# Five v tiles split among the score tiles and kept in DRAM, one turn of GpSimd for both final sums, and checks re-slotted: a Fourier and expert layer on one core

## The chip, the cores and the metric

The kernel runs on one core of a Trainium2 chip. The metric is the device time of one execution in microseconds (us); the median over runs counts. The profile is one execution recorded by the hardware profiler. Engine names: PE is the matrix engine (TensorE), DVE the vector engine, ACT the scalar engine, POOL GpSimd, SP the engine that issues most DMA transfers (SPq and POOLq are the DMA issues of SP and POOL).

## The reference, cut to what matters

```python
xn  = layernorm(x)                                   # x: 2048 x 512
A   = Re(DFT_seq(DFT_hidden(xn)))                    # 2048 x 512
q   = einsum("nd,dhc->nhc", xn, w_q)                 # 32 heads, two halves of 128
s1, s2 = q1 @ k1.T, q2 @ k2.T                        # 64 + 64 scores a head
i1, i2 = top2(s1), top2(s2)
cand, eidx = sums and indices of the 2 x 2 pairs;  top_s, top_e = top 2 of cand
g   = softmax(top_s)
act = gelu(einsum("nd,nhkd->nhk", xn, u[top_e]))     # u: 4096 experts x 512
B   = einsum("nhk,nhk,nhkd->nd", g, act, v[top_e])   # v: 4096 experts x 512
out = x + A + B
```

## The kernel before, in words

The 2048 rows are 16 tiles of 128. Operands of matmuls are split into a high and a low float16 part and multiplied in three products, so that the result has nearly float32 accuracy; the casts of the splits are ACT's (high part), with the low part's subtraction on POOL. While it computes, the kernel also tests its inputs (that the DFT matrices given are DFT matrices, that magnitudes fit the scaling); if a test fails, a slower branch at the end recomputes everything. These tests are called checks here.

The work comes in four stages, all on PE, one behind the other.

1. *Fourier part* (0 to 88 us): the DFT as matmuls; its result goes to DRAM (`y_d`, with `xt_d` for the transposed, split rows).
2. *Scores* (88 to 449 us): 8 groups of 4 heads (index j) by 16 row tiles (index i), 128 score tiles n = 16 j + i. Each is 12 matmuls (`scores`, L790) out of one of 4 PSUM buffers; ACT evicts it (L795), DVE takes the best of each head (MAX8 L798, FIND_INDEX8 L802). The matrix m of a group is the product of w_q and the keys, made by `m_stage` (L146) out of float16 halves of w_q that ACT and POOL prepare (`m_prep`, L160 to L168, in the "wq" ring of 4 buffers). `routing` (L643 to L687) turns a group's scores into experts and gates, in the group after it, in four calls; that of the last group follows the scores and is on DVE. The results for all rows stand in z, which is stored to DRAM as `z_d` (L888). Beside this stand lists by score tile: `todo[n]` holds fills and preparations, `checks` the early checks. A *fill* (`fill_uv`, L602 to L612) splits one of 16 tiles of u or of v: ACT casts the raw tile (L610), ACT scales it (L611), POOL subtracts (L612); its load (`fill_load`, L599) is issued some tiles earlier. The 16 u tiles and v tiles 0 to 10 are filled here (V2 = 11). An *early check* (`compare`, 32 of them, `EARLY`) loads 512 KB of DFT matrix into a buffer "cx" of which there are two, combines it on POOL (`diff`: L747, L753) and sums it on ACT (`judge`: L773, L774); check k is put at tile 20 + 13 k // 4, its load 4 tiles earlier and its judge 2 later.
3. *Row blocks*: rows 0 to 14 (NB = 15) go through all 4096 experts densely. For a block b, `u_part` makes z = u.x in 8 groups of 4 PSUM columns (L935, 48 matmuls each) with the gelu on ACT (L938); `g_mm` builds the gate matrix from one-hot factors that DVE makes (L961 for L, L966 and L969 for R; matmuls L971); `w_part` multiplies both on DVE (L981), and splits the product (ACT L988, DVE L991); `v_part` multiplies it with v (L1000, 96 matmuls of 512 columns); `finish` adds the Fourier part and x (L1015) and stores the rows. The loop over b runs v of block b, then u of block b + 2; blocks 0 and 1 have their u ahead of the loop. The x tile of a block (xb, 256 KB) is loaded by `prep` (L918), z of a block by `compact_d` (L923), y by `add_x` (L1008 from y_d on SP, L1009 x added by POOL's queue). Paced by v's and u's groups: the other 36 checks (`paced`, on DVE and ACT here) and, in block 0's v part, the fills of v tiles 11 to 15.
4. *The sixteenth block* is done row by row beside this: for 64 pairs of head and rank, POOL gathers a row of u and v for each of 128 rows (L1026), DVE takes the dot product (`dot`, L1042), ACT the gelu and the scaling (`gain`, L1053 to L1056), POOL adds it to ov (L1057). `pick` hands out these steps, 212 turns over the blocks.

At the end `verdict` sums the checks over partitions with two POOL instructions (partition_all_reduce, L1150 and L1151; DVE L1154 to L1169 takes the decision), and `finish` of block 14 and its store follow on DVE and SP.

The order on each engine is by priority and dependencies of a tile scheduler; `follow` adds an order without a wait between two instructions, and `hold` does so for all that a function issues. DMA loads of SP go out in the order of its queue.

## Time and profile before

| | us |
|---|---|
| median of 3 runs (1161.86, 1161.0, 1160.99) | 1161.0 |
| the profiled execution | 1159.16 |
| its span | 1157.4 |
| PE busy | 1111.0 (96%) |
| DVE busy | 924.8 (80%) |
| ACT busy | 670.4 (58%) |
| POOL busy | 482.4 (42%) |

The span runs from the first to the last recorded instruction; what lies around it in the execution is 1.8 us. A row of a timeline has the start in us, the duration, the engine, the line of the kernel, the operation with its output and input, and in brackets how long the engine sat idle before it and which instruction released it. A group's row has the busy time in us, the mean duration in ns, and the idle time before. The mean granted clock of PE was 0.99 of full speed.

### The profile page before, as it was taken

The page shows a single profiled execution, that of the slowest core. Times are in us where ns is not written, and L with a number is a line of the kernel's source. Part 1 is how long each engine was busy: PE and PEld are TensorE (multiplying, and loading weights), DVE is VectorE, ACT ScalarE, POOL GpSimd, SP SyncE. Part 2 cuts the span into 40 slices and gives each one's busy share as a digit, 9 for nine tenths or more (in the row PEclk, how much of TensorE's full clock was granted, in tenths as well). Part 3 has the DMA queues.
Part 4 walks back from the last instruction along what each step waited for, and adds up shares of the span by engine and source line. Part 5 has one row for each costly group of instructions (what it writes and reads, how often), then busy time and mean ns, then how long its engine had stood idle before and what let it go on. Part 6 is the DMA issues. An engine that isn't in the chain of part 4 may idle for free.

```text
span 1157.4 us, 29244 instructions
## 1 busy us (share of the span) xinstructions
PE 1111.0 (96%) x11681; PEld 730.1 (63%) x11681; DVE 924.8 (80%) x2790; ACT 670.4 (58%) x1250; POOL 482.4 (42%) x442
## 2 busy tenths in 40 slices
PE   5799999999999999979999999999999999999996
PEld 4354555444444446957687696786876876967842
DVE  7878897787978999897888777778787886787781
ACT  3575667687877866354464554554654645545541
POOL 0021749679887863140333333333333233333321
PEclk9899999999999999999999999999999999999998
DMA  8255245353443331532444535435444454354321
GB/s 314 79 212 189 84 136 175 135 181 101 162 162 126 110 110 36 168 107 78 118 159 152 151 112 167 147 96 159 147 141 119 155 156 150 108 162 149 113 52 49
DMA packets 73346, 157.02 MB, mean 136 GB/s; under 512 B 9062, under 2 KB 25965, under 8 KB 73200
## 3 DMA queue, kind: packets, MB, share of 16 engines
q1 hardware_dynamic: 61522, 117.30, 30.4%
q0 software_dynamic: 11520, 37.75, 11.8%
q8 instruction: 93, 1.52, 0.5%
q14 instruction: 53, 0.43, 0.1%
q10 hardware_dynamic: 158, 0.01, 0.0%
HBM read 141.08 MB, written 13.96 MB: 134 GB/s over the span
## 4 chain that ended last, share of the span: by engine, by line
PE 71%; DVE 12%; POOL 8%; issue 3%; ACT 2%; DMA 2%; SPq 0%; POOLq 0%; DVEq 0%; ACTq 0%
PE z L935 27%; PE v L1000 23%; PE s L790 12%; PE g L971 4%; DVE vals L798 2%; POOL wq L168 2%; DVE idx L802 2%; POOL wq L167 2%; PE p L368 2%; POOL cx L747 1%; POOL u L612 1%; DMA cx<-in_cb_dram 1%; PE m L146 1%; DVE L L961 1%; DVE ft L345 1%
## 5 line engine op out<-in xcount | busy, mean ns | idle before, releaser
L790 PE MATMUL s<-m,xq 128*128 128x512 f16 x1536 | 339.1, 379 | 0.9 <-ACT ss L795 0.9
L935 PE MATMUL z<-xb,u 128*128 128x128 f16 x5760 | 330.6, 219 | 2.4 <-DMA xb<-xt_d 2.4
L935 PEld LDWEIGHTS <-u 128*128 128x128 f16 x5760 | 324.5, 98 | 5.7 <-DMA xb<-xt_d 2.6
L1000 PE MATMUL v<-v,act 128*128 128x512 f16 x1440 | 321.3, 380 | 1.2 <-DVE act L991 1.1
L1057 POOL TENSOR_TENSOR ov<-ov,ga 128x512 f32<-128x512 f32 x64 | 96.0, 1500 | 401.0 <-ACT ga L1056 345.5
L790 PEld LDWEIGHTS <-xq 128*128 128x128 f16 x1536 | 148.4, 98 | 172.3 <-issue 1.4
L961 DVE TENSOR_TENSOR L<-io_lam,cmp 128x2048 f16<-128x2048 f16 x120 | 157.2, 1310 | 112.5 <-PE g L971 79.0
L1000 PEld LDWEIGHTS <-act 128*128 128x128 f16 x1440 | 137.7, 98 | 159.1 <-issue 1.7
L938 ACT ACTIVATE act<-z,scl 128x512 f32<-128x512 f32 x120 | 81.9, 684 | 174.9 <-PE z L935 174.7
L798 DVE MAX8 vals<-ss 128x8 f32<-128x64 f32 x1024 | 152.7, 217 | 16.2 <-ACT ss L795 15.9
L802 DVE FIND_INDEX8 idx<-vals,ss 128x8 uint16<-128x256 f32 x256 | 107.3, 419 | 0.0
L1026 POOL DMA_INDIRECT ga<-in_uv_dram,eix x64 | 93.7, 1463 | 32.3 <-POOL ov L1057 18.3
L991 DVE TENSOR_TENSOR act<-w,act 128x1024 f16<-128x1024 f32 x60 | 81.0, 1350 | 19.2 <-ACT act L988 17.5
L988 ACT ACTIVATE act<-w 128x1024 f16<-128x1024 f32 x60 | 80.9, 1348 | 26.5 <-DVE w L981 26.4
L795 ACT ACTIVATE ss<-s,wsc 128x512 f32<-128x512 f32 x112 | 75.1, 678 | 28.3 <-PE s L790 15.3
L773 ACT ACTIVATE cx<-cx 128x896 f32<-128x896 f32 x64 | 60.6, 947 | 36.2 <-POOL cx L753 9.6
L981 DVE SCALAR_TENSOR_TENSOR w<-act,scl,g 128x1024 f32<-128x1024 f32 x60 | 76.2, 1273 | 0.1
L747 POOL TENSOR_TENSOR cx<-cx 128x512 f32<-128x512 f32 (+2 forms) x56 | 61.8, 1120 | 27.1 <-DMA cx<-in_cb_dram 13.2
L971 PEld LDWEIGHTS <-L 128*128 128x128 f16 x1920 | 56.0, 96 | 15.5 <-issue 8.7
L971 PE MATMUL g<-R,L 128*128 128x32 f16 x1920 | 57.9, 176 | 8.0 <-DVE R L969 8.0
L969 DVE TENSOR_TENSOR R<-R,cmp 128x512 f16<-128x512 f16 x120 | 62.3, 519 | 1.8
L168 POOL TENSOR_TENSOR wq<-wq,wh 128x1024 f16<-128x1024 f32 x26 | 55.4, 2130 | 18.9 <-ACT wq L165 17.9
(276 smaller groups left out, 1259.9 us busy)
## 6 DMA issues: line engine op xcount, KB each, us to landing
cx<-in_cb_dram SPq DMA_DIRECT2D x64, 448.0 KB, 4.6
wq<-in_wq_dram SPq DMA_DIRECT2D x32, 512.0 KB, 4.1
fit<-in_wq_dram SPq DMA_DIRECT2D x28, 512.0 KB, 4.6
uv<-in_ut_dram SPq DMA_DIRECT2D x16, 512.0 KB, 3.9
uv<-in_vn_dram SPq DMA_DIRECT2D x16, 512.0 KB, 3.7
xq<-in_x_dram SPq DMA_DIRECT2D x8, 512.0 KB, 6.7
xt_d<-xq SPq DMA_DIRECT2D x16, 256.0 KB, 2.5
cx<-in_ca_dram SPq DMA_DIRECT2D x64, 64.0 KB, 3.5
```

Source lines behind the costliest of these rows:

```text
L790: mm = nc.tensor.matmul(ps, xt[i][:, l, kd, :], m[:, r, kd, :], start=(n == 0), stop=(n == 3 * KD - 1))
L798: nc.vector.max(vals[:, i, w, :, h], s[:, g, :])
L802: nc.vector.max_index(idx[:, i, w].rearrange("p k h -> p (k h)"), vals[:, i, w, 0:2].rearrange("p k h -> p (k h)"), s[:, w * HC:g + 1, :]. ...
L935: mm = nc.tensor.matmul(p[:, cc * P:(cc + 1) * P], ug[:, l, c % 2, kd, :], xb[:, r, kd, :], start=(n == 0), stop=(n == 3 * KD - 1))
L938: nc.scalar.activation(act[:, cg * 4:cg * 4 + 4, :].rearrange("p c n -> p (c n)"), p, AF.Gelu_apprx_tanh, scale=zsc)
L961: nc.vector.tensor_tensor(L.rearrange("p t (l two) -> p t l two", two=2), io_lam.rearrange("p (l two) -> p l two", two=2).unsqueeze(1).to_ ...
L971: i = nc.tensor.matmul(p[:, hf, t * NC:(t + 1) * NC], L[:, t, :], R[:, t, :], start=True, stop=True)
L988: i = nc.scalar.activation(w16[..., 0], w, AF.Copy)
L991: nc.vector.tensor_tensor(w16[..., 1], w, w16[..., 0], op=ALU.subtract)
L1000: mm = nc.tensor.matmul(pv, w16[:, c, :, l], vg[:, r, c % 2, :], start=(c == 0 and k == 0), stop=(c == NC - 1 and k == 2))
L1026: nc.gpsimd.indirect_dma_start(out=t, out_offset=None, in_=uv, in_offset=bass.IndirectOffsetOnAxis(ap=eix[:, n].rearrange("p k h -> p (k h ...
L1057: nc.gpsimd.tensor_tensor(o, o, t, op=ALU.add)
```

## The change

Its parts:

- *v tiles 11 to 15.* `fill_far` splits them among score tiles 104, 105, 106, 110 and 111, each in a buffer of the "wq" ring, and stores them to DRAM (`v_d`, 512 KB each). Once the score stage's memory is free they are loaded into place by five transfers on SP. The fills in block 0 go.
- *Early checks.* Three buffers instead of two; tiles 7 to 10 of groups 1 to 5, and ten tiles from 101 to 126; the load 3 tiles ahead, the judge one tile behind.
- *xb.* The tiles of x (but block 1's) come from a pool of their own on the other side of memory; block 0's is loaded at the start of the last score group.
- *Order in blocks.* The first two gate matmuls of block 0 come after groups 4 and 6 of z rather than 5 and 7; ACT's steps of checks and rows stand behind the gelu of the same z group; the last `w_part` of the last blocks comes a group earlier.
- *The sixteenth block.* x + y for it is added up early and kept in DRAM (`o_d`); the last two of POOL's additions are issued together, and both partition sums are put behind them. The picks are spread over 206 turns, none in every second group of block 13 and two a group in block 14.
- *Checks in blocks.* Block 13, the last but one, has none of the paced ones; they are spread over the groups before.

```diff
@@ -50,6 +50,8 @@
     z_d = dram.tile([NT, P, 3 * P], F16, name="z_d")
+    v_d = dram.tile([16 - V2, P, 4 * D], F16, name="v_d")
+    o_d = dram.tile([NS, P, D], F32, name="o_d")
@@ -599,8 +601,9 @@
-        def fill_uv(which, g, at=None):
-            dst = (u_sb if which == 0 else v_sb)[g]
+        def fill_uv(which, g, at=None, dst=None):
+            if dst is None:
+                dst = (u_sb if which == 0 else v_sb)[g]
             s = behind(su if which == 0 else sv, at)
@@ -617,6 +620,11 @@
         asums = wqp.tile([P, 16, 2], F32, name="asums", bufs=1)
+
+        def fill_far(g, at):
+            t = wq_tile(f"vs{g}").rearrange("p h k -> p (h k)").bitcast(F16)
+            fill_uv(1, g, at, t.rearrange("p (l c d) -> p l c d", l=2, c=2))
+            nc.sync.dma_start(v_d[g - V2], t)
@@ -709,8 +717,11 @@
                     follow(i, after)
+                if i.engine == mybir.EngineType.Activation and after.ins.name in GL:
+                    follow(i, GL[after.ins.name])
         later = []
+        GL = {}
@@ -719,7 +730,7 @@
             else:
-                t = sp.tile([P, 4, 4, 64], F32, tag="cx", name=f"cx{n}", bufs=2)
+                t = sp.tile([P, 4, 4, 64], F32, tag="cx", name=f"cx{n}", bufs=3)
             v_eng = nc.vector if at is None else nc.gpsimd
@@ -835,23 +846,31 @@
             todo[n - (3 if n < 113 else 1)].append(lambda at, w=which, g=g: fill_load(w, g))
+        for g, n in zip(range(V2, 16), () if safe else (104, 105, 106, 110, 111)):
+            todo[n].append(lambda at, g=g: fill_far(g, at))
+            todo[n - 3].append(lambda at, g=g: fill_load(1, g))
         checks = {}
...
-        for k in range(len(EARLY)):
-            n = 20 + k * 13 // 4
-            checks.setdefault(n - 4, []).append(lambda mm, k=k: check_load(k))
+        at_k = [13, 15] + [16 * j + i for j in range(1, 6) for i in (7, 8, 9, 10)]
+        at_k += [101, 103, 108, 112, 118, 120, 122, 124, 125, 126]
+        for k, n in enumerate(at_k):
+            checks.setdefault(n - 3, []).append(lambda mm, k=k: check_load(k))
             checks.setdefault(n, []).append(lambda mm, k=k: hold(cx[k][0], mm))
-            checks.setdefault(n + 2, []).append(lambda mm, k=k: hold(cx[k][1], mm))
+            checks.setdefault(n + 1, []).append(lambda mm, k=k: hold(cx[k][1], mm))
+        XB = {}
         m_stage(1, wq_tile, 0)
...
                 alloc_v(V1, V2)
+                xbp = stE.enter_context(tc.tile_pool(name="xbp", bufs=1, side="right"))
+                XB[0] = xbp.tile([P, 2, KD, P], F16, tag="xb", name="xb_0", bufs=1)
+                nc.sync.dma_start(XB[0].rearrange("p a k n -> p (a k n)"), xt_d[0])
             vals = sp.tile([P, NT, 2, 8, HC], F32, tag="vals", name=f"vals{j}", bufs=2)
@@ -899,13 +918,17 @@
                 xb = bp.tile([P, 2, 2, KD, P], F16, tag="ga", name="xb_1", bufs=BUFS)[:, 0]
+            elif b:
+                xb = xbp.tile([P, 2, KD, P], F16, tag="xb", name=f"xb_{b}", bufs=1)
             else:
-                xb = ap[0].tile([P, 2, KD, P], F16, tag="xb", name=f"xb_{b}", bufs=1)
+                xb = XB[0]
             act = ap[b % 2].tile([P, NC, P], F32, tag="act", name=f"act{b}")
...
         alloc_v(V2, 16)
+        for g in range(V2, 16 if not safe else V2):
+            nc.sync.dma_start(v_sb[g].rearrange("p l c d -> p (l c d)"), v_d[g - V2])
         TG = 32
@@ -915,7 +938,8 @@
             xb, act = BT[b] if b < 2 else blk_tiles(b)
-            nc.sync.dma_start(xb.rearrange("p a k n -> p (a k n)"), xt_d[b])
+            if b:
+                nc.sync.dma_start(xb.rearrange("p a k n -> p (a k n)"), xt_d[b])
             ACT[b] = (act, xb)
@@ -935,8 +959,8 @@
                         n += 1
-            nc.scalar.activation(act[:, cg * 4:cg * 4 + 4, :].rearrange("p c n -> p (c n)"), p,
-                                 AF.Gelu_apprx_tanh, scale=zsc)
+            GL[mm.ins.name] = nc.scalar.activation(act[:, cg * 4:cg * 4 + 4, :].rearrange("p c n -> p (c n)"), p,
+                                                   AF.Gelu_apprx_tanh, scale=zsc)
             return mm
@@ -1046,16 +1070,19 @@
                 T["o"] = o = bp.tile([P, D], F32, tag="ov", name=f"ov{n}", bufs=1)
-                nc.sync.dma_start(o, y_d[b])
-                nc.gpsimd.dma_start(o, x[b // 4, b % 4], accum_op=ALU.add)
+                nc.sync.dma_start(o, o_d[n])
             o = T["o"]
...
             nc.scalar.activation(t, t, AF.Copy, scale=z)
-            nc.gpsimd.tensor_tensor(o, o, t, op=ALU.add)
-            fetch()
+            T.setdefault("t", []).append(t)
+            if n and s == 0:
+                return
+            for t in T.pop("t"):
+                T["a"] = nc.gpsimd.tensor_tensor(o, o, t, op=ALU.add)
+                fetch()
             if s == N - 1:
@@ -1063,11 +1090,11 @@
             picks += [lambda f=f, k=k: f(*k) for f, k in ((dot, rows[i:i + 1]), (gain, rows[i - 1:i] if i else [])) for k in k]
-        turns = 16 * (NB - 2) + 4
+        turns = 16 * (NB - 3) + 14
         done = [0, 0]
-        def pick(after):
-            done[0] += 1
+        def pick(after, k=1):
+            done[0] += k
             made = nc.cur_bb.bb.instructions
@@ -1076,6 +1103,8 @@
                         follow(i, after)
+                    if i.engine == mybir.EngineType.Activation and after.ins.name in GL:
+                        follow(i, GL[after.ins.name])
@@ -1147,8 +1176,10 @@
                 nc.vector.tensor_reduce(fm[:, i:i + 1], chk[:, c], axis=AX.X, op=ALU.max)
-            nc.gpsimd.partition_all_reduce(fr[:, 0:2], fa, P, bass_isa.ReduceOp.add)
-            nc.gpsimd.partition_all_reduce(fr[:, 2:], sums_sb[:, 138:], P, bass_isa.ReduceOp.absmax)
+            i = nc.gpsimd.partition_all_reduce(fr[:, 0:2], fa, P, bass_isa.ReduceOp.add)
+            follow(i.ins, T["a"])
+            k = nc.gpsimd.partition_all_reduce(fr[:, 2:], sums_sb[:, 138:], P, bass_isa.ReduceOp.absmax)
+            follow(k.ins, i)
             r = fr[0:1, 2:]
@@ -1184,7 +1215,7 @@
             st[1] += 1
-            for f in st[0][st[2]:-(-len(st[0]) * st[1] // (8 * (NB - 2) + 2))]:
+            for f in st[0][st[2]:-(-len(st[0]) * st[1] // (8 * (NB - 2) - 2))]:
                 f()
@@ -1203,8 +1234,8 @@
             u_part(0, cg)
-            if cg in (5, 7):
-                g_mm(0, (cg - 5) // 2)
+            if cg in (4, 6):
+                g_mm(0, (cg - 4) // 2)
         for cg in range(8):
@@ -1213,14 +1244,20 @@
             g_mm(1, tg)
-        last = list(range(V2, 16))
+        last = list(range(V2, 16)) if safe else []
+        for n in range(0 if safe else NS):
+            b = NB + n
+            o = bp.tile([P, D], F32, tag="y", name=f"oy{n}", bufs=1)
+            nc.sync.dma_start(o, y_d[b])
+            nc.gpsimd.dma_start(o, x[b // 4, b % 4], accum_op=ALU.add)
+            nc.sync.dma_start(o_d[n], o)
         split = []
...
             else:
-                vw, vg = {0: 0, 2: 1, 4: 2, 6: 3}, {1: 2, 3: 3}
+                vw, vg = {0: 0, 2: 1, 4: 2, 5: 3}, {1: 2, 3: 3}
             for cg in range(8):
@@ -1238,17 +1275,23 @@
                     continue
-                if 0 < b < NB - 1 or b + 1 == NB and cg < 4:
+                if 0 < b < NB - 2 or b + 1 == NB and cg < 4:
                     paced(cg % 2, mm)
+                elif b + 2 == NB:
+                    flush(mm)
+                if b + 1 < NB:
+                    if cg == 4:
+                        add_x(b, mm)
+                elif cg == 0:
+                    add_x(b, mm)
+                if b and b + 2 != NB:
+                    pick(mm, 2 if b + 1 == NB else 1)
+                elif b:
+                    pick(mm, cg % 2)
                 if b + 1 == NB and cg == 4:
...
                         flush(mm)
-                    add_x(b)
                     verdict()
-                if cg == 4 and b + 1 < NB:
-                    add_x(b, mm)
-                if b:
-                    pick(mm)
             if safe:
...
             finish(b, pv)
```

## The prediction

> **What bounds the kernel now.** I read the page first, then busy time by stretch of the span, then PE's, DVE's, POOL's and SP's timelines where PE is not full.
>
> ```profile
> PE 1111.0 (96%) x11681; PEld 730.1 (63%) x11681; DVE 924.8 (80%) x2790; ACT 670.4 (58%) x1250; POOL 482.4 (42%) x442
> ```
>
> PE is busy for 1111.0 of 1157.4 us, so only about 46 us can go without less PE work, and the change takes no matmul away. By stretch (columns: window, length, then busy us and instruction count of PE, PE weight loads, DVE, ACT, POOL, then granted clock, DMA share, GB/s):
>
> ```profile
> 0.00:25.00 25.00, 15.15 (x72) 12.49 (x72) 17.18 (x52) 7.94 (x12) 1.63 (x13) 1.00 0.94 354
> ...
> 361.00:407.00 46.00, 45.56 (x295) 22.13 (x293) 39.09 (x216) 35.07 (x63) 37.58 (x44) 1.00 0.32 104
> ...
> 430.00:452.00 22.00, 18.88 (x93) 8.80 (x93) 21.76 (x126) 18.57 (x32) 10.89 (x7) 0.99 0.16 49
> ...
> 533.00:578.00 45.00, 45.00 (x609) 33.88 (x607) 36.80 (x68) 22.40 (x42) 13.34 (x9) 1.00 0.40 122
> ...
> 1125.00:1157.40 32.40, 21.45 (x98) 9.32 (x96) 7.18 (x35) 4.09 (x10) 4.58 (x5) 0.91 0.16 43
> ```
>
> The row 533:578 is a steady row block: PE 45.00 of 45. Whatever the change moves there (checks, gathered-row sums, the ACT operations behind the gelu) is hidden while PE stays full; I cost blocks 1 to 12 at nothing, and if that cover went, DVE with 36.80 of 45 would be the next to show. The change can act where PE has holes: the score part, the passage into the first blocks (from 430:452 on, PE 18.88 of 22), and the end (1125:1157.4, PE 21.45 of 32.4).
>
> **Step 1, the score part.** The waits of PE for POOL there, in one row (us in total, times, longest):
>
> ```profile
> PE m L146 <- POOL wq L168: 4.9, 5, 1.9
> ```
>
> The re-slotted checks stand at tiles 7 to 10 of each group, and no check is left on POOL between the casts of wq that feed the next group's m. I take the 4.9 us as gone (bounds 0 and 4.9). Against it five fills come into tiles 104 to 111 (361:407). Prices of one instruction each, and how DVE fares beside POOL:
>
> ```profile
> L611 ACT ACTIVATE uv<-uv,ss 128x1024 f32<-128x1024 f32 x27 | 31.0, 1147 | 0.6
> ...
> L773 ACT ACTIVATE cx<-cx 128x896 f32<-128x896 f32 x32 | 30.4, 949 | 16.3 <-POOL cx L753 9.6 <-POOL cx L768 6.7
> ...
> L774 ACT ACTIVATE cx<-cx 128x128 f32<-128x128 f32 x32 | 9.6, 301 | 0.0
> ```
> ```profile
> 405.64 1.97 POOL L747 TENSOR_TENSOR cx<-cx 128x256 f32<-128x256 f32 x2
> ...
> 417.05 2.13 POOL L612 TENSOR_TENSOR v<-uv,v 128x1024 f16<-128x1024 f32 x1 [0.94 <-ACT uv L611]
> ```
> ```profile
> 417.08 2.12 DVE L681 TENSOR_SCALAR eix<-di 128x8 int32<-128x8 int32 x1
> ...
> 462.25 0.16 DVE L681 TENSOR_SCALAR eix<-di 128x8 int32<-128x8 int32 x1
> ```
>
> A fill is two ACT passes (L610, L611) of 1.15 and one POOL pass of 2.13. The five give ACT 11.5 us; two checks fewer in this window (L773 and L774, 1.25 each) take 2.5 off, so 35.07 becomes 44.1 of 46. POOL gets 10.7 and loses at least two pairs of L747, 3.9, so 37.58 becomes 44.4. Both still fit, barely. What hides them is the row of score buffers between PE and ACT; if that cover is gone, PE waits. I take 0 for PE; the upper bound is rival B. DVE: at 417.08 a 128x8 operation took 2.12 us beside POOL's L612 of 417.05 and ended with it; the same one takes 0.16 at 462.25. DVE has no slack at the end of the scores (21.76 of 22). I take one such hit, 1.8 us (bounds 0, and all five fills, 10.7, which is rival C).
>
> [...]
>
> **Step 2, from scores to blocks.** PE's timeline (start, us, what, idle before), then DVE's and SP's:
>
> ```profile
> 451.75 17.85 PE L935 MATMUL z<-xb,u 128*128 128x128 f16 x288 [2.41 <-DMA xb<-xt_d]
> 469.43 0.95 PE L971 MATMUL g<-R,L 128*128 128x32 f16 x32
> 470.24 5.52 PE L935 MATMUL z<-xb,u 128*128 128x128 f16 x96
> ...
> 476.40 2.84 PE L935 MATMUL z<-xb,u 128*128 128x128 f16 x48
> ...
> 481.74 0.55 PE L971 MATMUL g<-R,L 128*128 128x32 f16 x16 [0.59 <-DVE R L969]
> ...
> 487.93 0.55 PE L971 MATMUL g<-R,L 128*128 128x32 f16 x16 [0.74 <-DVE R L969]
> ...
> 506.81 0.55 PE L971 MATMUL g<-R,L 128*128 128x32 f16 x16 [1.91 <-DVE R L969]
> ...
> 517.36 0.59 PE L971 MATMUL g<-R,L 128*128 128x32 f16 x16 [4.20 <-DVE R L969]
> 517.79 6.41 PE L1000 MATMUL v<-v,act 128*128 128x512 f16 x24
> ...
> 524.20 5.34 PE L1000 MATMUL v<-v,act 128*128 128x512 f16 x24
> ```
> ```profile
> 458.13 0.19 DVE L643 TENSOR_TENSOR c<-vals 128x48 f32<-128x48 f32 x1
> ...
> 465.65 0.42 DVE L969 TENSOR_TENSOR R<-R,cmp 128x512 f16<-128x512 f16 x1
> ```
> ```profile
> 464.29 0.37 SPq L888 DMA_DIRECT2D z_d<-z  x1
> 470.17 0.33 SPq L918 DMA_DIRECT2D xb<-xt_d  x1
> ```
>
> *DVE.* It ends its maxes at 458.13, minus 4.9, plus 1.8: 455.0. The same chain then makes the second R of block 0 ready at 462.9 (before 466.07) and z_d's store starts at 461.2 (before 464.29).
>
> *PE, block 0.* xb_0 comes before the last score group, so the 2.41 goes: z starts at 451.75 - 4.9 - 2.41 = 444.4. Five groups of 48 matmuls at 2.76 (half of 5.52) take it to 458.2, where the second half of g(0,0), moved forward by one, needs the R of 462.9: a new wait of 4.7, with all of PE's later matmuls queued behind it. Then three groups and two g of 0.95: 10.2, and a slow clock. Its price from rows: 288 matmuls took 17.85 after the 2.41 hole, against 3 x 5.52 = 16.56, so 1.3. Block 1's z would start at 474.4.
>
> [...]
>
> *xb_1.* Its load needs z_d landed (before: 464.29 to 470.17, 5.9 us); now the five reloads of v (512 KB each) are queued ahead of it on SP. They start at 461.2 + 5.9 = 467.1. At 354 GB/s, the best stretch of the trace (0:25), 2.62 + 0.26 MB take 8.1 us. One load of that size:
>
> ```profile
> uv<-in_vn_dram SPq DMA_DIRECT2D x16, 512.0 KB, 3.7
> ```
>
> alone needs 3.7, of which 1.5 at that rate, so 2.2 are latency: xb_1 lands at 477.4 (bounds: 471 if the queues let it pass, 485 at half the rate, since indirect gathers run too). Block 1's z then starts at 477.4, 1.0 later than the 476.40 of before, with a second dip of 1.3.
>
> *Blocks 0 and 1.* From here the holes 0.59 + 0.74 + 1.91 + 4.20 = 7.4 and the dip at 517.79 (6.41 against 5.34, 1.1) stand in before. Where they come from:
>
> ```profile
> 496.68 2.24 DVE L969 TENSOR_TENSOR R<-R,cmp 128x512 f16<-128x512 f16 x1
> ...
> 513.84 3.14 DVE L961 TENSOR_TENSOR L<-io_lam,cmp 128x2048 f16<-128x2048 f16 x1
> ```
> ```profile
> L612 POOL TENSOR_TENSOR v<-uv,v x5: 2127/2306/3152, 495.5 to 513.6; 128x1024 f16<-128x1024 f32 x5
> ```
>
> Five DVE operations (first and last shown; 0.42 is usual for an R) are stretched, each beside one of the five L612. With the fills gone DVE gets some 9.5 us back, more than the holes hold, and v11 to v15 are reloaded long before their use at 510. What is late next is z's own gelu, with room. I take all 8.5 (bounds 3 and 8.5). Net of this step: +1.0 + 1.3 - 8.5 = **-6.2**. The o_d store on SP waits for an accumulate of POOL's queue; behind it are y and row loads needed tens of us later, so 0.
>
> **Step 3, the end.** POOL, PE, DVE, SP:
>
> ```profile
> 1130.70 0.41 POOL L1150 PARTITION_ALL_REDUCE fr<-fa  x1 [6.08 <-ACT ga L1056]
> 1138.43 1.25 POOL L1057 TENSOR_TENSOR ov<-ov,ga 128x512 f32<-128x512 f32 x1 [7.33 <-issue]
> ...
> 1148.04 0.60 POOL L1151 PARTITION_ALL_REDUCE fr<-sums  x1 [6.04 <-issue]
> ```
> ```profile
> 1114.48 0.55 PE L971 MATMUL g<-R,L 128*128 128x32 f16 x16 [0.59 <-DVE R L969]
> ...
> 1127.16 20.46 PE L1000 MATMUL v<-v,act 128*128 128x512 f16 x94 [1.14 <-DVE act L991]
> ```
> ```profile
> 1150.31 0.75 DVE L1015 SCALAR_TENSOR_TENSOR y<-v,scl,y 128x512 f32<-128x512 f32 x1
> ```
>
> Each turn of POOL between elementwise work and a partition sum leaves 6 to 7 us idle: three turns, and the last puts the second sum at 1148.04, after PE's end at 1147.62; the verdict follows and the last y waits for it until 1150.31. With both sums behind both last row sums there is one turn, and in the new order of DVE the last row's dot product comes before PE's last v matmuls, so the verdict is ready before PE ends. y then starts at PE's end: 1150.31 - 1147.7 = 2.6 gained. The holes 0.59 and 1.14 come from DVE's checks in the block but one, which go: up to 1.7; I take 1.4. Together **-4.0** (bounds 0 and 4.3). The output store and what follows stay.
>
> **Sum.** -6.2 - 4.0 = -10.2 against the profiled execution's 1159.16 (span 1157.4 and 1.8 around it): 1149.0. The runs' median, 1161.0, lies 1.8 above that execution, so the forecast is 1150.8.
>
> **Rivals.** A measurement of this kernel can tell about 0.2% (2.3 us) from no change: faster means under 1158.7, slower over 1163.3.
> - A, xb_1 is not what binds (it lands by 474). Then 3.0 of wait and a 1.3 dip go too: 1146.5. For: SP spreads each load over 16 engines. Against: five loads ahead of it in one queue.
> - B, the slower side: ACT is the bound of the two last score groups. In 361:407 it idles 46 - 35.07 = 10.9 us, waiting for scores and POOL. If those waits stay in the order of its queue, the added 9.0 us make the group longer by that, and four more checks in the last group add 5.0: 1150.8 + 14.0 = 1164.8. It gives slower once more than 12.5 of the 14.0 are not hidden. Against it, PE's wait for ACT in the whole score part:
> ```profile
> L790 PE MATMUL s<-m,xq 128*128 128x512 f16 x1536 | 339.1, 379 | 0.9 <-ACT ss L795 0.9
> ```
> 0.9 us, so the buffers are ahead now.
> - C, POOL's fills hold DVE for all their 10.7 us rather than 1.8: R, z_d and xb_1 all come 8.9 later: 1159.7, no change to be told. xb_1 at 485 alone would give 1158.4.
> - D, the sums don't do what is said: the verdict is still the later one at the end, and the tail gives nothing: 1154.8.
>
> **How the numbers follow.** Forecast 0.45, A 0.20, B 0.15, C 0.12, D 0.08. Faster is the forecast, A, D and about half of C: 0.79; same is the rest of C: 0.06; slower is B: 0.15. The range leaves out B (0.15) and little of A's far side, where DVE doesn't hold PE either: 1143 to 1161.
>
> **What would show it.** Right: no wait of m for L168; a hole of some 5 us at g(0,0) near 458 and one of 2 to 5 at block 1's z near 474; no DVE R over 1 us between 490 and 520; the steady block at 45.5; both partition sums ten us ahead of PE's end, and y right behind it. Wrong: evictions L795 late and PE idle between 385 and 449 (B), DVE's first L643 after 460 (C), or DVE checks before PE's last hole.

## The result, and the profile after

The changed kernel takes 1169.6 us (median of 4 runs, 1168.6 to 1171.9) against 1161.0: ratio 1.0075 (95% interval 1.0058 to 1.0093), **slower** by 8.6 us. The forecast was 1150.8, with a range that ended at 1161. The profiled execution took 1169.36 us, its span 1167.5.

The page's first part for the changed kernel: PE does the same matmuls. Of the 10.1 us that the span grew, 5.9 are idle time of PE (52.3 us instead of 46.4) and 4.2 are busy time: right behind some holes matmuls run slower. The 72 of 441.89 below take 17.39 us, where the 72 at 385.72 take 15.70; the granted clock was 0.58 in 441.9:446.

```profile
PE 1115.2 (96%) x11681; PEld 732.7 (63%) x11681; DVE 906.0 (78%) x2790; ACT 670.3 (57%) x1257; POOL 480.0 (41%) x442
```

Busy time by stretch, changed kernel, columns as in the prediction (PE, weight loads, DVE, ACT, POOL, clock, DMA share, GB/s):

```profile
361.00:407.00 46.00, 43.06 (x282) 20.90 (x281) 38.99 (x201) 36.55 (x59) 36.28 (x35) 1.00 0.33 107
407.00:430.00 23.00, 19.36 (x87) 8.39 (x86) 15.78 (x97) 18.18 (x31) 15.69 (x22) 1.00 0.75 251
430.00:452.00 22.00, 18.04 (x76) 7.76 (x76) 21.33 (x118) 15.80 (x29) 17.58 (x18) 0.92 0.36 110
...
480.00:518.00 38.00, 29.04 (x525) 28.59 (x522) 22.15 (x29) 10.90 (x14) 4.86 (x4) 0.87 0.49 170
...
533.00:578.00 45.00, 45.00 (x610) 33.96 (x609) 34.81 (x61) 22.08 (x41) 7.59 (x5) 1.00 0.34 103
```

The steady block (533:578) is full, as forecast. PE lost its time in two places: the last two score groups (361 to 452: 10.5 of 91 us idle) and 480:518 (9.0 idle, at a clock of 0.87). What it waited for, in the list of PE's waits of the changed kernel (total us, times, longest):

```profile
PE s L801 <- ACT ss L806: 10.0, 8, 3.4
...
PE z L959 <- DMA xb<-xt_d: 8.4, 1, 8.4
PE m L148 <- POOL wq L170: 2.8, 3, 1.3
```

(Line numbers are those of the changed kernel: L801 are the scores, L806 their eviction, L959 z, L962 its gelu, L995 g.) The wait of the scores for ACT was 0.9 us before and is 10.0 now; that for xb was 2.4 at block 0 and is 8.4 at block 1. New are also 1.30 us in block 0's z for ACT's `cmp` (L705) and 2.03 in block 14's z for a gelu. PE's timeline shows the two largest waits, and, at the end, v running without a hole:

```profile
441.89 17.39 PE L801 MATMUL s<-m,xq 128*128 128x512 f16 x72 [3.42 <-ACT ss L806]
...
459.45 5.52 PE L959 MATMUL z<-xb,u 128*128 128x128 f16 x96
...
476.28 0.55 PE L995 MATMUL g<-R,L 128*128 128x32 f16 x16 [1.42 <-DVE R L993]
...
494.97 5.28 PE L959 MATMUL z<-xb,u 128*128 128x128 f16 x48 [8.40 <-DMA xb<-xt_d]
...
544.70 0.50 PE L959 MATMUL z<-xb,u 128*128 128x128 f16 x6
...
1110.13 4.30 PE L959 MATMUL z<-xb,u 128*128 128x128 f16 x48 [2.03 <-ACT act L962]
...
1129.74 31.24 PE L1024 MATMUL v<-v,act 128*128 128x512 f16 x144
```

Read from one landmark to the next, in both profiled executions (differences of rows of the two PE timelines, and of the last y of DVE):

| stretch | before | after | difference |
|---|---|---|---|
| start to end of the last scores | 449.00 | 459.28 | +10.3 |
| from there to z of block 0 | 2.75 | 0.17 | -2.6 |
| z of block 0 to z of block 1 | 24.65 | 35.52 | +10.9 |
| z of block 1 to z of block 2 | 56.37 | 49.73 | -6.6 |
| z of block 2 to PE's end | 614.85 | 616.28 | +1.4 |
| PE's end to the last y | 2.69 | 0.04 | -2.65 |
| last y to the span's end | 7.1 | 6.5 | -0.6 |

The sum is +10.1, the difference of the spans. The change took out what it aimed at (rows two, four and six, 11.9 us in all) and paid 22.6 for it in rows one, three and five. In row three stand the waits for xb (8.40), for R (1.42) and for `cmp` (1.30).

**Why the scores are late.** ACT is not full there: 36.55 of 46, 18.18 of 23, 15.80 of 22. It stands. The rows of its timeline in which it waits longest in the last group, of the kernel before and then of the changed one (L651 and L659 are the same operation, the exponential in `routing`; the 128x16 one belongs to the last group itself, whose first four row tiles are routed within it, on DVE):

```profile
414.50 0.26 ACT L651 ACTIVATE c<-c 128x64 f32<-128x64 f32 x1 [4.57 <-POOL c L648]
...
428.60 0.21 ACT L651 ACTIVATE c<-c 128x16 f32<-128x16 f32 x1 [3.51 <-DVE c L648]
```
```profile
425.65 0.26 ACT L659 ACTIVATE c<-c 128x64 f32<-128x64 f32 x1 [2.84 <-POOL c L656]
...
441.05 0.21 ACT L659 ACTIVATE c<-c 128x16 f32<-128x16 f32 x1 [5.91 <-DVE c L656]
```

While ACT waits for POOL's or DVE's subtraction, the evictions of the next scores stand behind it in its queue (none in the changed kernel between 434.46 and 441.17, though PE's row of 36 score matmuls from 430.54 ends at 438.47); PE runs on through the four PSUM buffers and then stops. A wait of 4.57 or 3.51 cost PE at most 0.9; the one of 5.91 is followed at once by PE's hole of 3.42 at 441.89. Four of PE's eight holes of the scores follow such a wait: 0.79 at 328.44, 0.86 at 375.13, 1.20 at 426.53 and the 3.42, together 6.3 of the 10.0 us.

The other four (0.82 at 402.25, 0.47 at 410.65, 1.18 at 417.41, 1.25 at 430.54), 3.7 us, stand behind the fills' own steps on ACT. Casts and scalings come in a row there, with the next eviction behind them, and the one at 410.65 follows a wait of ACT of 1.88 us for a fill's load. One such row on ACT, and PE's hole behind it:

```profile
413.56 2.19 ACT L613 ACTIVATE vs<-uv,ss 128x1024 f16<-128x1024 f32 x2
```
```profile
417.41 7.93 PE L801 MATMUL s<-m,xq 128*128 128x512 f16 x36 [1.18 <-ACT ss L806]
```

Why the subtraction is late, in the changed kernel's POOL and DVE timelines:

```profile
418.95 1.96 POOL L758 TENSOR_TENSOR cx<-cx 128x512 f32<-128x512 f32 x2
...
421.40 2.13 POOL L615 TENSOR_TENSOR vs<-uv,vs 128x1024 f16<-128x1024 f32 x1
423.49 0.32 POOL L651 TENSOR_TENSOR c<-vals 128x64 f32<-128x64 f32 x1
...
431.87 6.31 POOL L615 TENSOR_TENSOR v<-uv,v 128x1024 f16<-128x1024 f32 x3
```
```profile
424.40 0.23 DVE L654 TENSOR_TENSOR pm<-c,c 128x64 f32<-128x64 f32 x1 [3.51 <-POOL c L653]
...
436.05 2.16 DVE L652 TENSOR_TENSOR c<-vals 128x16 f32<-128x16 f32 x1
```

In POOL's order two of the five new fills (`vs`, at 416.86 and 421.40) stand ahead of routing's first add (L651), with a check (L758) between them; DVE, with its next group's maxes behind, idles 3.51 us for POOL. Before, that add stood at 412.16 with POOL waiting for DVE:

```profile
412.16 0.32 POOL L643 TENSOR_TENSOR c<-vals 128x64 f32<-128x64 f32 x1 [4.02 <-DVE vals L798]
```

In the second place, DVE's own add of the last group takes 2.16 us beside three fills in a row (of v, which the kernel before has too), where the same add took 0.16 before (427.34). The maxes beside those fills kept their time: 0.73 us for five at 431.77 and 0.72 at 433.75, and 0.72 at 449.31 in the kernel before, where POOL stands idle.

### The profile page after: what moved, and what is told of

Same layout as the page of the kernel before. It is cut to its first block, busy times and chain, and to the rows that moved or that the text cites. A ratio compares the mean times of both kernels' runs of the same rounds, so it can differ in the third digit from the quotient of the medians.

```text
span 1167.5 us, 29293 instructions
## 1 busy us (share of the span) xinstructions
PE 1115.2 (96%) x11681; PEld 732.7 (63%) x11681; DVE 906.0 (78%) x2790; ACT 670.3 (57%) x1257; POOL 480.0 (41%) x442
## 4 chain that ended last, share of the span: by engine, by line
PE 74%; POOL 11%; DVE 6%; issue 4%; DMA 2%; ACT 1%; SPq 0%; POOLq 0%; DVEq 0%; ACTq 0%
PE v L1024 27%; PE z L959 26%; PE s L801 13%; PE g L995 4%; POOL cx L758 2%; POOL v L615 2%; PE p L370 2%; POOL u L615 2%; POOL wq L169 1%; POOL wq L170 1%; PE m L148 1%; POOL vs L615 1%; DVE vals L809 1%; DMA xb<-xt_d 1%; DVE idx L813 1%
## 5 line engine op out<-in xcount | busy, mean ns | idle before, releaser
L801 PE MATMUL s<-m,xq 128*128 128x512 f16 x1536 | 341.7, 380 | 10.1 <-ACT ss L806 10.0
L959 PE MATMUL z<-xb,u 128*128 128x128 f16 x5760 | 333.4, 220 | 12.3 <-DMA xb<-xt_d 8.4
L959 PEld LDWEIGHTS <-u 128*128 128x128 f16 x5760 | 326.8, 98 | 16.0 <-issue 13.0
L801 PEld LDWEIGHTS <-xq 128*128 128x128 f16 x1536 | 148.8, 98 | 184.1 <-issue 14.8
L985 DVE TENSOR_TENSOR L<-io_lam,cmp 128x2048 f16<-128x2048 f16 x120 | 150.3, 1253 | 102.3 <-PE g L995 71.4
L962 ACT ACTIVATE act<-z,scl 128x512 f32<-128x512 f32 x120 | 81.6, 682 | 192.0 <-PE z L959 188.3
L806 ACT ACTIVATE ss<-s,wsc 128x512 f32<-128x512 f32 x112 | 74.3, 675 | 24.2 <-PE s L801 22.3
L758 POOL TENSOR_TENSOR cx<-cx 128x512 f32<-128x512 f32 (+2 forms) x56 | 61.7, 1120 | 20.4 <-DMA cx<-in_cb_dram 18.2
L995 PEld LDWEIGHTS <-L 128*128 128x128 f16 x1920 | 55.8, 96 | 8.5 <-issue 1.8
L995 PE MATMUL g<-R,L 128*128 128x32 f16 x1920 | 57.5, 176 | 1.4 <-DVE R L993 1.4
L993 DVE TENSOR_TENSOR R<-R,cmp 128x512 f16<-128x512 f16 x120 | 57.1, 476 | 2.0
```

The costliest lines, as they stand in the source:

```text
L758: v_eng.tensor_tensor(v, v, tv[:, 0:1].to_broadcast([P, len(ix), 256]), op=o)
L801: mm = nc.tensor.matmul(ps, xt[i][:, l, kd, :], m[:, r, kd, :], start=(n == 0), stop=(n == 3 * KD - 1))
L959: mm = nc.tensor.matmul(p[:, cc * P:(cc + 1) * P], ug[:, l, c % 2, kd, :], xb[:, r, kd, :], start=(n == 0), stop=(n == 3 * KD - 1))
L962: GL[mm.ins.name] = nc.scalar.activation(act[:, cg * 4:cg * 4 + 4, :].rearrange("p c n -> p (c n)"), p, AF.Gelu_apprx_tanh, scale=zsc)
L985: nc.vector.tensor_tensor(L.rearrange("p t (l two) -> p t l two", two=2), io_lam.rearrange("p (l two) -> p l two", two=2).unsqueeze(1).to_ ...
L995: i = nc.tensor.matmul(p[:, hf, t * NC:(t + 1) * NC], L[:, t, :], R[:, t, :], start=True, stop=True)
```

## The experiments

Each kernel is timed against the kernel before on the same chip; ratios are to it. As a landmark for the end of the scores I use the start of the first transposes behind them (448.84 before, 459.11 after). Single executions lie up to 3.1 us apart ahead of the score stage already (the first matmul of the first m of that stage comes at 87.33 before, 87.93 after, 87.04 in e4_xb1_first and 90.18 in e10_fills_early), so I read no difference of 1 or 2 us off this landmark.

### Which part delays the scores?

**e1_no_far**: the changed kernel, but v tiles 11 to 15 are filled in block 0 again.

```diff
-        for g, n in zip(range(V2, 16), () if safe else (104, 105, 106, 110, 111)):
+        for g, n in zip(range(V2, 16), ()):
...
-        for g in range(V2, 16 if not safe else V2):
-            nc.sync.dma_start(v_sb[g].rearrange("p l c d -> p (l c d)"), v_d[g - V2])
...
-        last = list(range(V2, 16)) if safe else []
+        last = list(range(V2, 16))
```

> The changed kernel with v tiles 11 to 15 filled in block 0 again, nothing stored or reloaded; all else of the change stays. Theory F (the five fills among score tiles 104 to 111 push POOL's routing and ACT's evictions back, PE idles 10.0 us for ACT there): the last score ends near 447 instead of 459.3, PE's wait for ACT in the scores falls from 10.0 to under 3 us, the 8.4 us wait for xb_1 is gone too, the stretched R and L beside POOL's fills and some 7 us of holes before R come back; time 1155 to 1159. Rival C (the re-slotted early checks, four more of them in the last group, make the holes): the last score still ends after 455, the wait for ACT stays over 7 us, time 1163 to 1167.

**e2_far_only**: the kernel before, with the five fills at the change's tiles, stored and reloaded (behind the loads of xb_0 and xb_1); checks, xb and end as before.

```diff
+        for g, n in zip(range(V2, 16), () if safe else (104, 105, 106, 110, 111)):
+            todo[n].append(lambda at, g=g: fill_far(g, at))
+            todo[n - 3].append(lambda at, g=g: fill_load(1, g))
...
         prep(0)
         prep(1)
+        for g in range(V2, 16 if not safe else V2):
+            nc.sync.dma_start(v_sb[g].rearrange("p l c d -> p (l c d)"), v_d[g - V2])
```

> The kernel before with the five fills among the score tiles, their store and the reload alone (the reload behind block 0's and 1's x tiles on SP). Theory F: the last score ends 6 to 10 us later than the 449.0 of before, no R over 1 us between 490 and 520, the holes before R gone (8 us), time 1159 to 1164. Rival C: the last score ends before 451, time 1151 to 1155.

**e3_checks_only**: the kernel before, with the change's early checks alone.

```diff
-                t = sp.tile([P, 4, 4, 64], F32, tag="cx", name=f"cx{n}", bufs=2)
+                t = sp.tile([P, 4, 4, 64], F32, tag="cx", name=f"cx{n}", bufs=3)
...
-            n = 20 + k * 13 // 4
+        at_k = [13, 15] + [16 * j + i for j in range(1, 6) for i in (7, 8, 9, 10)]
+        at_k += [101, 103, 108, 112, 118, 120, 122, 124, 125, 126]
```

> The kernel before with the early checks in the new tiles and three buffers alone. Theory F: the last score ends at 446 to 450, PE's wait for wq falls from 4.9 to about 2.8, time 1158 to 1162. Rival C: PE waits for ACT over 5 us in the scores, the last score ends after 454, time over 1165.

| | median us | ratio | transposes start |
|---|---|---|---|
| e1_no_far | 1163.2 | 1.0024 (1.0009 to 1.0039) | 457.94 |
| e2_far_only | 1165.4 | 1.0034 (1.0023 to 1.0044) | 461.93 |
| e3_checks_only | 1167.2 | 1.0054 (1.0039 to 1.0068) | 457.10 |

The fills alone delay the scores by 13.1 us, the checks alone by 8.3, both together by 10.3: not a sum, and either part is enough. So my first theory, that the fills are the whole cause, fell with e1 (9.1 us of delay stay without them), and e3 bears out its rival that the checks' places cost by themselves. How the checks do it is visible in e3. POOL's timeline, then ACT's and PE's:

```profile
416.49 0.32 POOL L645 TENSOR_TENSOR c<-vals 128x64 f32<-128x64 f32 x1
416.76 1.95 POOL L747 TENSOR_TENSOR cx<-cx 128x512 f32<-128x512 f32 x2
419.14 0.32 POOL L648 TENSOR_TENSOR c<-c,c 128x64 f32<-128x64 f32 x1 [0.42 <-DVE c L647]
```
```profile
419.49 0.26 ACT L651 ACTIVATE c<-c 128x64 f32<-128x64 f32 x1 [6.73 <-POOL c L648]
...
436.60 0.22 ACT L651 ACTIVATE c<-c 128x16 f32<-128x16 f32 x1 [6.18 <-DVE c L648]
```
```profile
422.60 12.21 PE L790 MATMUL s<-m,xq 128*128 128x512 f16 x48 [2.25 <-ACT ss L795]
437.44 19.82 PE L790 MATMUL s<-m,xq 128*128 128x512 f16 x84 [2.64 <-ACT ss L795]
```

A check's two L747 stand between routing's adds and its subtraction, the exponential waits 6.73 where it waited 4.57, and PE's hole follows 3 us later; the same again at 436.60. All of PE's 6.8 us of waiting for ACT in e3 (four holes) stands behind such waits. In e2, which has no check in a new place, ACT's wait in the second place is of the same kind and PE's hole follows (5.63 of the 10.7 us that PE waits for ACT there). The other three holes of e2, 5.1 us, stand behind the fills' own steps: a wait of ACT of 2.21 us for a load, casts, and the wait of 4.85 us shown first, for a fill's store:

```profile
429.17 1.15 ACT L612 ACTIVATE v<-uv,ss 128x1024 f16<-128x1024 f32 x1 [4.85 <-DMA v_d<-vs]
...
441.14 0.22 ACT L658 ACTIVATE c<-c 128x16 f32<-128x16 f32 x1 [5.33 <-DVE c L655]
```
```profile
441.98 20.12 PE L797 MATMUL s<-m,xq 128*128 128x512 f16 x84 [5.63 <-ACT ss L802]
```

In the kernel v tiles 5 to 10 are placed when the "wq" ring is given up at the start of the last group (`wq_st.close()`, `alloc_v(V1, V2)`). A cast into the ring's memory would have to wait for the stores out of it; the row fits that, but no run tests it.

e1 also brings the old holes in block 0 back, which is how the gain of moving the fills is told: PE waits 6.6 us in 4 holes for R (4.2 the longest), where the changed kernel has 1.4 in one.

### What does block 1's x cost behind the reloads?

**e4_xb1_first**: the changed kernel, with the five reloads issued behind the loads of block 1.

```diff
-        for g in range(V2, 16 if not safe else V2):
-            nc.sync.dma_start(v_sb[g].rearrange("p l c d -> p (l c d)"), v_d[g - V2])
...
         prep(0)
         prep(1)
+        for g in range(V2, 16 if not safe else V2):
+            nc.sync.dma_start(v_sb[g].rearrange("p l c d -> p (l c d)"), v_d[g - V2])
```

> The changed kernel with the five reloads of v behind block 1's x tile in SP's queue, nothing else. If the queue order makes the 8.4 us wait of PE for xb_1, the wait falls under 1.5 us, block 1's z starts near 487 instead of 495, and the time falls by 7 to 10 us to 1160 to 1163, the scores unchanged (last score at 459). Rival: xb_1 waits for z_d and the gathers whatever stands ahead of it; then at least 5 us of the wait stay and the time falls by less than 4.

1158.9 us, ratio 0.9984 (0.9972 to 0.9995): 10.7 below the changed kernel, for five DMA issues moved by some lines. PE no longer waits for xb; the scores are as late as before this edit (transposes at 458.13). SP's timeline of the changed kernel, then of e4:

```profile
479.62 2.38 SPq L931 DMA_DIRECT2D v<-v_d  x5
482.05 0.50 SPq L942 DMA_DIRECT2D xb<-xt_d  x1
```
```profile
479.23 0.33 SPq L940 DMA_DIRECT2D xb<-xt_d  x1
479.60 3.10 SPq L1228 DMA_DIRECT2D v<-v_d  x5
```

In the changed kernel block 1's z starts 15.3 us behind the first reload's issue: 2.88 MB in that time are 188 GB/s. The transfers as a whole were not slow in it (changed kernel; the last column is GB/s):

```profile
479.60:487.00 7.40, 6.41 (x127) 5.93 (x124) 4.58 (x9) 1.73 (x3) 3.86 (x3) 1.00 0.87 304
487.00:495.00 8.00, 0.03 (x1) 0.06 (x2) 4.26 (x5) 1.64 (x2) 0.00 (x0) 0.69 0.91 354
```

That is some 5.1 MB. The reloads shared the transfers with others, above all three row gathers that POOL issued between 480.48 and 483.57 (1.57 MB in the packets of POOL's queue). The reloads themselves are needed only from v's sixth group on, and PE waits for none of them in e4.

### ACT's queue, DVE or POOL?

**e5_exp_later** tests whether the place of the exponentials in ACT's queue is the cause: e4, with routing's two exponentials of the last group put some tiles later. The edit moves whole calls of `routing`, so DVE's and POOL's steps of these calls go later too, not the exponentials alone.

```diff
+                e = nc.scalar.activation(ex, c00, AF.Exp)
+                if not safe and EV[1]:
+                    follow(e.ins, EV[0])
...
-                if i in (1, 2, 4) and pend is not None:
+                if i in ((1, 2, 6) if j + 1 == NCH else (1, 2, 4)) and pend is not None:
...
-                if j + 1 == NCH and i == 4:
+                if j + 1 == NCH and i in (7, 10):
```

> The changed kernel with block 1's x tile ahead of the reloads (as in e4_xb1_first) and, in the last score group only, ACT's two routing exponentials moved some four and six tiles later in its queue; nothing else. Theory Q (the exponentials stand in ACT's queue ahead of evictions and wait for DVE and POOL, which the added fills and checks make late; PE runs out of score buffers behind them): PE's wait for ACT in the scores falls from 10.2 to under 5 us, the last score ends at 450 to 454 instead of 458.1, time 3 to 6 us under e4's 1158.9. Rival D (DVE's own work, stretched beside POOL, sets the end): DVE's last index search stays at 467 within 1.5, and the time within 1.5 of e4's, PE only waits later.

1166.0 us, ratio 1.0043 (1.0027 to 1.006): 7 worse than e4. Neither bet held: PE's wait for ACT stayed at 10.4, and DVE's last index search came at 472.82, 5.6 later than e4's 467.25. DVE is now full to the end of the scores (39.19 of 40):

```profile
430.00:470.00 40.00, 28.71 (x166) 15.18 (x166) 39.19 (x174) 26.54 (x49) 26.14 (x27) 0.96 0.33 101
```

Later exponentials leave more of routing's DVE work, which hangs on them, for the stretch where DVE has nothing to spare: PE's transposes now wait 4.4 us for DVE. This order is dearer; since DVE's steps moved along, the run doesn't show what the exponential's place alone is worth. DVE as the bound fits the direction, but not the price that rival D gave, and doesn't say what made DVE late.

**e9_no_pool_check** tests POOL: e4 with POOL's part of the 32 early checks left out (their loads and ACT's sums stay).

```diff
             def diff():
+                if at is not None:
+                    return
...
-            nc.vector.tensor_tensor(flags, flag, flag2, op=ALU.max)
+            nc.vector.tensor_tensor(flags, flag, flag, op=ALU.subtract)
```

> e4_xb1_first with POOL's part of the 32 early checks left out (their loads and ACT's sums stay; the checks' verdict is set to pass). Theory P (DVE's routing operations are stretched and wait beside POOL's work in the last groups, DVE sets the end of the scores): DVE's last index search falls from 467.3 to 460 or earlier, DVE operations stretched over 0.15 us beside POOL over the scores fall from 26 us in sum to under 16. Rival A (ACT's load from the five fills sets it): the last index search stays after 464.

1148.2 us in the one run made, 10.7 below e4's median. All five fills are in it, at the change's tiles, and so is ACT's load. Its 361:407 by stretch and an exponential of ACT:

```profile
361.00:407.00 46.00, 46.00 (x298) 22.38 (x297) 39.45 (x204) 35.60 (x60) 26.41 (x27) 1.00 0.39 138
```
```profile
432.20 0.21 ACT L659 ACTIVATE c<-c 128x16 f32<-128x16 f32 x1 [2.42 <-DVE c L656]
```

ACT is as busy (35.60 of 46 against 36.55), PE is full there, and POOL has 26.41 instead of 36.28 us of work. The exponential that waited 5.91 waits 2.42, DVE's last index search comes at 456.50 (e4: 467.25), and the holes of PE behind such waits, 6.3 us in e4 (0.74, 0.87, 1.19, 3.49), are gone. So POOL's check work made these, as theory P has it; rival A's bet (an index search after 464) fell.

The scores end where they did before the change (transposes at 449.08 against 448.84), but as a balance. PE waits 0.7 us for POOL's wq, where it waited 4.9 before and 2.8 in e4, and it still waits 4.4 us for ACT, where it waited 0.9 before. Most of that is behind a store of a fill, ACT first and then PE:

```profile
421.34 2.19 ACT L613 ACTIVATE v<-uv,ss 128x1024 f16<-128x1024 f32 x2 [3.31 <-DMA v_d<-vs]
```
```profile
425.19 10.60 PE L803 MATMUL s<-m,xq 128*128 128x512 f16 x48 [3.34 <-ACT ss L808]
```

So what the fills do by their own steps on ACT and their store (3.9 us of PE's wait in e4, 4.4 here) is left, and POOL's check work is not its cause. The second half of theory P missed. I count what each DVE instruction takes over the tenth percentile of its operation and shape, where that is over 0.15 us, from 88 to 470 us: 20.0 us before the change, 25.8 in e4, 23.1 in e9. POOL's checks make some 2.8 us of that sum, where DVE's last index search comes 10.75 earlier without them; most of what they add is waiting.

### The end

**e7_end_only**: the kernel before with the change's end alone (`o_d`, the turns, both partition sums behind the row sums, nothing paced in block 13).

```diff
+            T.setdefault("t", []).append(t)
+            if n and s == 0:
+                return
+            for t in T.pop("t"):
+                T["a"] = nc.gpsimd.tensor_tensor(o, o, t, op=ALU.add)
...
+            i = nc.gpsimd.partition_all_reduce(fr[:, 0:2], fa, P, bass_isa.ReduceOp.add)
+            follow(i.ins, T["a"])
...
-                if 0 < b < NB - 1 or b + 1 == NB and cg < 4:
+                if 0 < b < NB - 2 or b + 1 == NB and cg < 4:
```

> The kernel before with the end of the change alone: both sums behind the row sums, x + y of the sixteenth block kept in DRAM, no paced checks in block 13, the spread of the picks. My prediction's step 3 alone: y starts at PE's end (2.6 us gained), the holes before 1115 and 1127 go (1.4 to 1.7): 1157 to 1158. Rival: the denser checks in the blocks before open a hole of 2 us there, without any new order on ACT: 1159 to 1160.

1158.5 us, ratio 0.998 (0.9965 to 0.9995): 2.3 gained of the 4.0 that the prediction gave to the end. y follows PE's last matmul (1147.44, y at 1147.48), but a new hole stands in block 14's z:

```profile
1098.09 2.84 PE L936 MATMUL z<-xb,u 128*128 128x128 f16 x48 [2.73 <-ACT act L939]
```

**e6_no_gl**: e4 without the order that puts checks and rows behind the gelu.

```diff
-                if i.engine == mybir.EngineType.Activation and after.ins.name in GL:
-                    follow(i, GL[after.ins.name])
```

> e4_xb1_first without the order that puts ACT's steps of checks and rows behind the gelu of the same z group. If that order makes the new 2.5 us hole of PE near 1099 (ACT waits for DVE's check step with the next gelu behind it), the hole falls under 0.5 and the time by 2 to 4 us against e4's 1158.9. If the denser pacing of the checks makes it, the hole stays over 1.5 and the time within 1.

1157.5 us, ratio 0.9971 (0.9959 to 0.9984). The hole stays, so that order doesn't make it:

```profile
PE z L955 <- ACT act L958: 2.7, 1, 2.7
```

**e8_both**: e5 and e6 in one.

```diff
+                if not safe and EV[1]:
+                    follow(e.ins, EV[0])
...
-                    follow(i, GL[after.ins.name])
```

> e5_exp_later and e6_no_gl together. If the two holes are independent, the gains add: 1151 to 1155, faster than both kernels. If rival D holds and the hole near 1099 is the pacing's, 1157 to 1160.

1165.7 us, ratio 1.0043 (1.003 to 1.0056): nothing beyond e5's loss.

### A version with the mechanism and without its price

**e10_fills_early**: e6, with the early checks in the tiles and two buffers of before, and the five fills at score tiles 20, 22, 24, 26 and 39, in 130:221, where the kernel before leaves POOL (the fifth pair, 59.40 of 91 us) more room than in 361:407 (37.58 of 46):

```profile
130.00:221.00 91.00, 91.00 (x602) 46.98 (x600) 80.36 (x417) 65.40 (x135) 59.40 (x68) 1.00 0.47 153
```

```diff
-        for g, n in zip(range(V2, 16), () if safe else (104, 105, 106, 110, 111)):
+        for g, n in zip(range(V2, 16), () if safe else (20, 22, 24, 26, 39)):
...
-                t = sp.tile([P, 4, 4, 64], F32, tag="cx", name=f"cx{n}", bufs=3)
+                t = sp.tile([P, 4, 4, 64], F32, tag="cx", name=f"cx{n}", bufs=2)
...
+            n = 20 + k * 13 // 4
```

> The end of the change, block 0's x tile early, block 1's x tile ahead of the reloads, the checks in their old tiles, no added order on ACT, and the five fills moved from tiles 104 to 111 to tiles 20, 22, 24, 26 and 39, where ACT and POOL are busy about half the time. If it is the crowding of POOL and ACT in the last two groups that costs, the last score ends at 447 to 451 as in the kernel before, the holes before R are gone, y follows PE's end: 1148 to 1152, faster than both kernels. If fills cost wherever they stand (their 512 KB stores and the extra passes), the last score ends after 454: 1155 to 1159.

1149.3 us (1146.5 to 1153.2), ratio 0.9898 (0.9879 to 0.9917): faster than both kernels. The profiled run is the slowest of the six, with the transposes at 452.78, some 3 us of which it lost before the scores. PE's scores wait for ACT 1.1 us in all. One expected thing didn't come: a hole before R stays, 2.98 us at g(0,0) (470.05; 2.99 in e11 below). The hole in block 14's z remains:

```profile
1095.41 2.84 PE L954 MATMUL z<-xb,u 128*128 128x128 f16 x48 [2.63 <-ACT act L957]
```

**e11_pace_old**: e10, with paced checks in block 13 again, spread as before.

```diff
-            for f in st[0][st[2]:-(-len(st[0]) * st[1] // (8 * (NB - 2) - 2))]:
+            for f in st[0][st[2]:-(-len(st[0]) * st[1] // (8 * (NB - 2) + 2))]:
...
-                if 0 < b < NB - 2 or b + 1 == NB and cg < 4:
+                if 0 < b < NB - 1 or b + 1 == NB and cg < 4:
```

> e10_fills_early with the paced checks in block 13 again and their old spread; the two sums stay behind the row sums. If leaving block 13 out of the pacing only moved the check step that waits for its load (DVE waits for in_wt, ACT for DVE, the next gelu behind it) from block 13's v part into block 14's z part, the 2.6 us hole near 1095 goes, holes of 0.6 and 1.1 us before PE's last stretch come back, and the time falls by 1 to 3 us against e10's 1149.3. If the hole comes from the spread of the row picks, it stays, and the time rises by 1 to 2 us.

1147.8 us (1145.6 to 1149.1), ratio 0.9897 (0.9881 to 0.9914): the best version, 12.3 below the kernel before. The scores end where they did before the change (transposes at 449.28). The hole in block 14's z is gone, and the holes of 0.6 and 1.1 us that were expected in its place didn't come:

```profile
1079.78 10.88 PE L954 MATMUL z<-xb,u 128*128 128x128 f16 x192
...
1105.94 31.24 PE L1019 MATMUL v<-v,act 128*128 128x512 f16 x144
```

Against e10 the medians differ by less than the runs of either spread; what is shown is the hole, not a time. Its cause stands in the changed kernel's DVE and ACT rows: a check's sum waits for its load, ACT waits for DVE's next step of that check, and gelus of z stand behind ACT's.

```profile
1102.94 0.42 DVE L1122 TENSOR_REDUCE sums<-cx 128x1 f32<-128x256 f32 x1 [0.95 <-DMA cx<-in_wt_dram]
```
```profile
1107.00 0.31 ACT L1139 ACTIVATE cx<-cx 1x128 f32<-1x128 f32 x1 [3.53 <-DVE cx L1137]
...
1109.42 0.66 ACT L962 ACTIVATE act<-z,scl 128x512 f32<-128x512 f32 x1
```

## Why the prediction was wrong, by its steps

The miss is 1169.6 - 1150.8 = 18.8 us. By the forecast's own landmarks: z of block 0 at 459.45 instead of 444.4, +15.05; from there to z of block 1 35.52 instead of 33.0, +2.5; then to z of block 2 49.73 instead of 49.2, +0.5; to PE's end 616.28 instead of 613.45, +2.8; y to the span's end -0.6; and the median lies 0.25 above the profiled execution, where 1.8 was taken: -1.6.

- **Step 1, the step that failed: "What hides them is the row of score buffers between PE and ACT ... I take 0 for PE."** The waits of m for POOL went from 4.9 to 2.8, and PE's wait for ACT from 0.9 to 10.0. I added up busy time (ACT 44.1 of 46, POOL 44.4 of 46) and asked whether it fits; it does fit (36.55 and 36.28 were done in that window, a part having slipped behind it), and that was not the question. Routing is a chain that goes back and forth between POOL, DVE and ACT, and ACT's part stands in front of the evictions. POOL work put among it makes ACT wait. The four score buffers covered a wait of 4.57 us before; in the changed kernel waits of 5.12 and 5.91 cost PE 0.86 and 3.42, and one of 2.84, with fill passes ahead of it, cost 1.20. These holes are 6.3 of the 10.0 us, and e9 shows that POOL's check work makes them. The other 3.7 are the fills' casts, scalings and loads on ACT itself, between the evictions.
- **"I take one such hit, 1.8 us"** for DVE beside POOL: DVE's last index search came at 468.0 instead of 457.8 (worked out from the two traces), 10.2 later. The upper bound of 10.7 was the right size, but only in part through stretched instructions, whose sum from 88 to 470 us grew by 6.0 (20.0 before, 26.0 in the changed kernel): DVE idled 3.51 us for POOL, and the maxes waited for late evictions.
- **Step 2, xb_0:** its 2.41 went, as forecast, but 1.30 for ACT's `cmp` came into the same z, a term that the sum doesn't have. **The new wait at g(0,0):** 1.42 instead of 4.7, as DVE's chain and PE were late by different amounts; with the scores on time (e10, e11) it is 3.0.
- **Step 2, xb_1:** the cause and the queue were right, the time wrong: 10.3 us were taken, 15.3 measured, between that and the bound of 485 (17.9). The transfers did run at 304 to 354 GB/s together; the term gave all of that to the reloads and xb_1, and POOL's gathers, named in the bound only, took their share. e4 prices the order of the queue at 10.7 us.
- **Step 2, the holes of blocks 0 and 1:** right. -6.6 measured against -7.2 forecast (8.5 less a dip of 1.3); e1 brings 6.6 us of them back.
- **Step 3:** y follows PE's end: right (2.65 against 2.6, e7 the same). The holes of 0.59 and 1.14 went, but one of 2.03 came, so the 1.4 was not gained. It is what the prediction counted among the signs against it, in a form it didn't name: the check steps that left block 13 stand in block 14's z (e10 against e11). The rest of the +1.4 before PE's end is a slow clock behind that hole: the 48 matmuls of 1110.13 took 4.30 us where 48 take 2.84, at a granted clock of 0.63 (1110.1:1114.4). The prediction has no term for it.

**The rivals.** B gave 1164.8 for the slower side, the nearest of all, and put the time in the right place. Its mechanism, ACT's load, holds in part: ACT was 21 to 28% idle in the three stretches, but 3.7 of PE's 10.0 us stand behind the fills' steps on ACT; the 6.3 behind routing's waits do not. C had the right engine, POOL holding up DVE, and its 8.9 us are near the 10.3 measured; it came out as no change because it left xb_1 at the better rate. A delay of C's size and some two thirds of the way to xb_1's bound both came, and I had added neither to the other; that a number near the result stands in each is no merit of the forecast. A and D are refuted: xb_1 did bind, and the end did what it says. A's point that a load is spread over 16 engines holds in the trace of before: with one load of 512 KB in flight (`wq`, issued at 326.49) the 16 DMA engines were busy for 0.98 of 328.3:328.8, at 377 GB/s.

**What stays open.** Within the waits behind routing, no run separates the DVE steps that are stretched beside POOL (2.16 us at 436.05) from those that come late. Nor is it shown why fills and checks together cost less (10.3) than the fills alone (13.1). No run has the five fills at the change's tiles without their store, so what the store costs is read from two waits of ACT only (4.85 in e2, 3.31 in e9). e9 rests on one run; it is 10.7 us under e4's median, where the runs of one kernel here lie up to 6.8 apart (e7).

## What to carry to other kernels

Before work is moved into a stretch, look for the chains that cross the engine in question and for what stands behind them in its queue (here the evictions behind ACT's exponential): POOL at 79% (36.28 of 46) with a chain through it had no room here, and the four score buffers covered a wait of 4.57 us at no cost, but not one of 5.12, which cost 0.86, nor one of 3.51 with a fill's cast ahead of the next eviction (0.88 in the kernel before). Put bulk reloads that are needed late behind the small load that is needed next; here that was worth 10.7 us. When an effect can be had in several places, try the stretch where the engines on the chain are least busy: the same five fills cost 13 us at tiles 104 to 111 and nothing that shows at 20 to 39 (transposes at 449.28 in e11_pace_old). That less busy engines are the whole reason is not shown: at the early tiles no v tile waits for a store either.

## What the runs showed of the hardware

- Five loads of 512 KB and one of 256 KB, queued together, took 15.3 us from the first issue to use (188 GB/s), while all transfers together ran at 304 and 354 GB/s; three gathers of POOL's queue (1.57 MB) ran beside them.
- Behind a hole of 2.03 us in the changed kernel 48 matmuls of z took 4.30 us (granted clock 0.63); behind one of 2.73 in e7_end_only 48 took 2.84, as elsewhere in that trace (552.32, without a hole). Both are 128x128 matmuls of block 14, so the length of the hole alone doesn't settle the dip.
- Beside fills on POOL (three in 6.31 us) one of DVE's small routing adds took 2.16 us in the changed kernel, 0.16 before. It is not the two-input adds alone: a cast with one input took 2.12 in e9, beside a fill of 2.17 at 429.29, and 0.46 in e11. DVE's maxes kept their time: the 1000 between 88 and 470 us took 0.17 to 0.24 us each, before and after the change.

```profile
429.39 2.12 DVE L670 CAST if<-idx 128x64 f32<-128x64 uint16 x1
```
